# Seeding a PSUM bank with the first product, and interleaving two gated-unit products, in a hedgehog-attention and GLU kernel

## The chip, the core and the metric

The kernel runs on one core of one Trainium2 chip. A core has a matrix engine (TensorE, PE in the profile), a vector engine (VectorE, DVE), a scalar engine (ScalarE, ACT), a general engine (GpSimd, POOL) and a queue engine that issues transfers (SyncE, SP). Matrix products are written to PSUM, which this kernel uses as eight banks of 128 partitions by 512 float32 values. All other tiles lie in SBUF. Each engine works through its own queue in order, and engines wait for each other by semaphores. The metric is the device time of one execution in microseconds; the time of a kernel is the median over runs.

## The reference, cut to what matters

```python
xn = layernorm(x)                                  # x: 2048 tokens x 1024
q, k, v = split_heads(xn @ wqkv)                   # 32 heads of 32
phi_q, phi_k = [concat(softmax(p), softmax(-p)) for p in (q @ w_phi, k @ w_phi)]
o = phi_q (phi_k^T v) / (phi_q (phi_k^T 1) + 1e-6)  # linear attention, per head
s = merge_heads(o) @ wo
h = sigmoid(xn @ w_gate) * (xn @ w_up)             # w_gate, w_up: 1024 x 3584
out = x + s * silu(h @ w_down)
```

All inputs and the result are float32.

## The kernel before, in words

Every large product is computed by a seven-product scheme: both factors are split into 2 x 2 blocks, and seven products of sums of blocks replace eight products of blocks. The seven are named B11, B21, T2, T3, T4, T1, B22 (line 52 and after). With the products written as names, the four blocks of a result are B11 + B21; u1 + T4; u2 + T1; u1 + T1 + B22, where u1 = B11 + T2 and u2 = u1 + T3. Every factor is split into a rounded part and a remainder (`split`: a ScalarE cast, then a VectorE subtraction), and each block product is three matmuls (`mm3`, lines 135 to 137), so that one product over 4 blocks of 128 in the contraction is 12 matmuls of 512 columns into one PSUM bank.

The tokens are worked in two chunks of 1024. For each chunk come first the projections V, K and Q, then the GLU's gate and up products; after both chunks the down products, and at the end the attention output with `wo`. The background work (features of queries, features and key-value sums of keys, the token-major normalization of chunk 1, sums of `wo` and `w_down` blocks) is taken from a list and put, task by task, behind an anchor instruction of the foreground (`background`): a task is planned only after the anchor. In chunk 1 of the GLU a task of key features comes every six products (`k_task`): two transfers, two VectorE reductions and two subtractions (`features`, L446 to L450), an Exp on ScalarE (L451) over 1024 columns, a reduction (L453), a reciprocal (L454), a multiplication (L467), the splits of the features (1024 columns) and of v (512 columns), and a running sum (L476). Its eight matmuls on the key-value banks (L486) are issued before the next task. In chunk 0 of the GLU the tasks are query features and the normalization.

Apart from the opening part (the list `FIRST`) and the last part (`PAIR`), where the order of every engine is written out, a planner sets the order: it takes the instructions in the order of the program and a model of their durations, and gives each engine its queue; a matmul whose operand or bank is not ready by the model is passed by others that are.

In a projection, one product is done for four token tiles, each in a bank of its own (`pbank`). The results are collected by `proj_out`: ScalarE copies B11 out to an SBUF tile u1p and B21's bank out to a result tile; VectorE adds T2's bank onto u1p, and likewise for T3, T4, T1 and B22. T2, T3 and T1 begin anew in the bank; B21, T4 and B22 accumulate on B11, T3 and T1.

In the GLU, one unit (j, s) is a pair of weight column blocks of the gate (s = 0) or of the up matrix (s = 1), and there are 14 x 2 units in a chunk. Its seven products are done in the order B11, T2, B21, T3, T1, T4, B22, with the four opening products B11, T2, T3, T1 each in the next of four banks. B11 is copied out by ScalarE (L1069); T2 (L1071), T3 (L1073) and the last three results (L1081 for the gate, L1088 for up) are added by VectorE; a gate result then goes through ScalarE's sigmoid (L1079 from the bank for B21, L1082 from SBUF for the others), an up result is multiplied with the stored gate, on VectorE for B21 (L1085) and on GpSimd for the other three (L1089). GpSimd then forms the sums of blocks that the down products take, and SP stores them.

The weight operands lie in a ring of eight slots, filled up to eight products ahead (`prep`). `glu_load` loads a unit's raw blocks and `glu_sums` forms their sums on GpSimd; in chunk 0 the split sums are also stored and in chunk 1 loaded back. Both functions are called when the first product of a unit is prepared.

Of the kernel before, what the change touches and what calls it, by code (L numbers as in the profile page):

```python
# [49 lines left out]
def hedgehog_glu_kernel(  # L50
# [77 lines left out]
    def split(o, src):  # L128

        nc.scalar.copy(o[0], src)  # L130
        return nc.vector.tensor_sub(o[1], src, o[0].bitcast(F32))  # L131
# [228 lines left out]
    def prep():  # L360
# [39 lines left out]
    last_evac = []  # L400

    def proj_out(c, which, i, u, b, held=None):
# [12 lines left out]
        def evac(y, x):  # L415
            last_evac[:] = [nc.vector.tensor_add(y, x, b).ins]
# [3 lines left out]
        elif i == B21:  # L420
            y = yp.next()
            nc.scalar.copy(y, b)
            store(0, 0, y)
        elif i == T2:
# [3 lines left out]
        elif i == T4:  # L428
            y = yp.next()
            evac(y, u1p[u])  # L430
            store(0, 1, y)
# [461 lines left out]
    def do_e(o, u):  # L893
        stores[o, u] = []
        proj_out(0, K if o[0] == "K" else V, product(o)[1], int(u), banks[int(u)], stores[o, u])
# [93 lines left out]
    gmm = Ring(banks[:4])  # L989
# [4 lines left out]
    gates = []  # L994
# [22 lines left out]
    for n, (kind, c, what, i) in enumerate(ops):  # L1017
# [3 lines left out]
        if kind == "proj":  # L1021
            for u in range(4):
                if i in opening:
# [3 lines left out]
                for k in range(4):  # L1027
                    mm3(pbank[u], (xo[:, k, 0, us], xo[:, k, 1, us]), pair(ws[k]),
                        i in opening and k == 0, k == 3, skip_group_check=True)
# [6 lines left out]
            if c and n - n1 in EARLY:  # L1036
                background(last_evac[0])
            if (i in (T2, T3, B22)) if c else n in (12, 14, 16, 18):
                with tc.issue_after(last_load[0]):
                    background(last_evac[0], bg2)  # L1040
# [4 lines left out]
        if (j, s, i) == (0, 0, 0):  # L1045
            step(1000)
        if i in opening:
            gbank[i] = gmm.next()
        bank = gbank[{B21: B11, T4: T3, B22: T1}.get(i, i)]
        w = [h.rearrange("p (k m) -> p k m", m=P) for h in pair(ws[0])]  # L1050
        xo = run(XO[i], 4)
        for k in range(4):
            mm3(bank, (w[0][:, k], w[1][:, k]), (xo[:, k, 0], xo[:, k, 1]),
                i in opening and k == 0, k == 3, skip_group_check=True)
# [3 lines left out]
        last_unit = u == len(units) - 1  # L1058
        if flow["item"] == len(items) and flow["made"] - flow["used"] < NW:
            hfree.append(ws[0])  # L1060
            if last_unit and i == 0:
                wfree.extend(range(16, 20))
            while wfree and down_prep():
                pass
        if i == B11:
            u1, u2 = ur.next(), ur.next()
            if s == 0:
                gates = [gates_r.next() for _ in range(4)]
            nc.scalar.copy(u1, bank)  # L1069
        elif i == T2:  # L1070
            v = nc.vector.tensor_add(u1, u1, bank)  # L1071
        elif i == T3:
            v = nc.vector.tensor_add(u2, u1, bank)  # L1073
        else:
            q = {B21: 0, T1: 3, T4: 2, B22: 1}[i]
            g = gates[q]
            if s == 0:
                if q == 0:
                    nc.scalar.activation(g, bank, AF.Sigmoid)  # L1079
                else:  # L1080
                    v = nc.vector.tensor_add(g, u2 if q == 3 else u1, bank)  # L1081
                    nc.scalar.activation(g, g, AF.Sigmoid)  # L1082
            else:
                if q == 0:
                    nc.vector.tensor_mul(g, g, bank)  # L1085
                else:
                    b = u1 if q == 1 else u2
                    v = nc.vector.tensor_add(b, u2 if q == 3 else u1, bank)  # L1088
                    nc.gpsimd.tensor_mul(g, g, b)  # L1089
                if q != 1:  # L1090
                    nc.sync.dma_start(h_d[(B11, None, B21, T4)[q], j, :, c], g)
                else:

                    a11, a21, a12, a22 = gates
# [8 lines left out]
        m = (u % (2 * NJ)) * 7 + glu_order.index(i)  # L1103
        if c == 0:
            if len(bg) > 2 * (TT + 3) and i == T2 and m > 7:
                background(v.ins)
        else:
            if m >= 1 and (m - 1) % 6 == 0:
                background(v.ins)
# [275 lines left out]
```

## Time and profile before

| quantity | value |
|---|---|
| median time of 3 runs | 2378.32 us (2374.84 to 2380.21) |
| profiled execution | span 2376.2 us from first to last instruction; the page gives no other time of it |
| PE busy | 2361.1 us, 99% of the span |
| VectorE busy | 1778.2 us, 75% |
| ScalarE busy | 1022.0 us, 43% |
| GpSimd busy | 959.8 us, 40% |
| granted TensorE clock | 1.000 (mean over the span) |

The profile shows one execution. Busy time of an engine is the union of its instructions' durations; "idle before" is the time that an engine stood still ahead of a group of instructions, with the instruction that released it behind an arrow. A line number like L131 is that of the helper which issues the instruction. Names of tiles are those of the program without numbers: `bank` is a PSUM bank, `w` the weight ring, `fa`, `fb`, `fc` raw and result tiles in SBUF, `p` the split features of keys. Matmuls are pipelined, so a row of 0.39 us can start every 0.23 us.

### The profile page before, as it was taken

Reading aid. Unit: us, or ns where it says so; the run is one execution under the profiler, and the core shown is the slowest. Engines: PE = TensorE matmul, PEld = TensorE weight load, DVE = VectorE, ACT = ScalarE, POOL = GpSimd, SP = SyncE. Lnnn points to the kernel's source line nnn. Section 1 sums busy time; section 2 is a strip of 40 time slices with the busy share of each in tenths; the row PEclk is TensorE's granted clock in tenths of the full one; section 3 lists DMA queues with packets and bytes.
Section 4 is the critical chain, followed back from the end, with each engine's and each line's share of the span. In section 5 each row is a group of like instructions: output and inputs, shape, how many; then the busy total and the mean of one; then the engine's idle time right before and its main releaser. Section 6 shows DMA issues by size and latency. Waiting matters only on the chain.

```text
span 2376.2 us, 31871 instructions
## 1 busy us (share of the span) xinstructions
PE 2361.1 (99%) x10972; PEld 1966.2 (83%) x10972; DVE 1778.2 (75%) x2340; ACT 1022.0 (43%) x1516; POOL 959.8 (40%) x613
## 2 busy tenths in 40 slices
PE   9999999999999999999999999999999999999999
PEld 8888888888888888888878888888888888888887
DVE  8626777877777575668884888865889998878776
ACT  7333344444434342324443444444444334455553
POOL 0223456666666433123443222232333334424566
PEclk9999999999999999999999999999999999999999
DMA  6689987778776787677777666668666666876665
GB/s 237 234 310 321 339 318 263 289 265 291 259 283 246 248 309 261 234 262 242 275 266 250 231 219 216 222 207 312 209 220 230 239 218 209 288 252 244 204 209 177
DMA packets 233587, 600.49 MB, mean 253 GB/s; under 512 B 30672, under 2 KB 30928, under 8 KB 228816
## 3 DMA queue, kind: packets, MB, share of 16 engines
q1 hardware_dynamic: 233424, 598.45, 72.3%
q8 instruction: 86, 1.41, 0.2%
q14 instruction: 77, 0.63, 0.1%
HBM read 363.20 MB, written 235.14 MB: 252 GB/s over the span
## 4 chain that ended last, share of the span: by engine, by line
PE 92%; DVE 4%; DMA 2%; issue 1%; ACT 1%; POOL 0%; SPq 0%; DVEq 0%; ACTq 0%
PE bank L135 29%; PE bank L137 29%; PE bank L136 29%; PE bank L696 1%; PE bank L672 1%; PE bank L486 1%; PE bank L285 1%; DMA fc<-wqkT 1%; DVE p L131 1%; DVE w L131 0%; DVE fc L450 0%; DVE fc L449 0%; DMA x<-x 0%; DMA fa<-wf_d 0%; DVE stk L453 0%
## 5 line engine op out<-in xcount | busy, mean ns | idle before, releaser
L136 PE MATMUL bank<-x,w 128*128 128x512 f32 x2352 | 915.7, 389 | 0.0
L135 PE MATMUL bank<-x,w 128*128 128x512 f32 x2352 | 909.8, 390 | 1.6 <-DVE fc L1073 1.1
L137 PE MATMUL bank<-x,w 128*128 128x512 f32 x2352 | 906.3, 390 | 0.0
L130 ACT CAST w<-fa 128x512 fp32r<-128x512 f32 (+1 forms) x430 | 294.8, 688 | 574.0 <-PE bank L136 365.9
L135 PEld LDWEIGHTS bank<-x,w 128*128 128x128 f32 x2352 | 441.6, 188 | 94.1 <-DVE fc L1073 2.3
L137 PEld LDWEIGHTS bank<-x,w 128*128 128x128 f32 x2352 | 441.5, 188 | 91.5 <-DVE w L131 0.4
L136 PEld LDWEIGHTS bank<-x,w 128*128 128x128 f32 x2352 | 441.6, 188 | 90.3
L131 DVE TENSOR_TENSOR w<-fa,w 128x512 fp32r<-128x512 f32 (+1 forms) x430 | 415.8, 972 | 104.1 <-ACT w L130 90.8
L135 PE MATMUL bank<-w,x 128*128 128x512 f32 x708 | 277.8, 393 | 0.2 <-ACT w L877 0.2
L136 PE MATMUL bank<-w,x 128*128 128x512 f32 x708 | 276.2, 390 | 0.9 <-DVE w L878 0.9
L137 PE MATMUL bank<-w,x 128*128 128x512 f32 x708 | 275.8, 390 | 0.0
L1089 POOL TENSOR_TENSOR fb<-fb,fc 128x512 f32<-128x512 f32 x57 | 89.0, 1561 | 291.6 <-DVE fc L1088 264.8
L137 PEld LDWEIGHTS bank<-w,x 128*128 128x128 f32 x708 | 132.9, 188 | 27.8 <-DVE x L868 0.3
L136 PEld LDWEIGHTS bank<-w,x 128*128 128x128 f32 x708 | 133.1, 188 | 27.4 <-DVE w L878 1.3
L135 PEld LDWEIGHTS bank<-w,x 128*128 128x128 f32 x708 | 133.1, 188 | 27.2 <-ACT w L877 0.6
L628 POOL TENSOR_TENSOR fc<-fc 128x1024 f32<-128x1024 f32 x32 | 81.4, 2542 | 173.7 <-ACT fc L451 125.4
L1088 DVE TENSOR_TENSOR fc<-fc,bank 128x512 f32<-128x512 f32 x84 | 57.5, 684 | 102.5 <-PE bank L137 97.4
L131 DVE TENSOR_TENSOR x<-fa,x 128x512 fp32r<-128x512 f32 x112 | 113.5, 1013 | 23.8 <-ACT x L130 23.6
L130 ACT CAST w<-fb 128x512 fp32r<-128x512 f32 x112 | 69.7, 622 | 141.7 <-PE bank L136 115.3
L131 DVE TENSOR_TENSOR p<-fc,p 128x1024 fp32r<-128x1024 f32 (+2 forms) x97 | 103.9, 1081 | 10.6 <-ACT p L130 8.3
L130 ACT CAST p<-fc 128x1024 fp32r<-128x1024 f32 (+2 forms) x97 | 70.7, 738 | 90.3 <-DVE fc L467 50.7
L640 POOL TENSOR_TENSOR fc<-fc,sa 128x1024 f32<-128x1024 f32 x32 | 70.4, 2199 | 90.6 <-DVE sa L637 90.6
(258 smaller groups left out, 3231.2 us busy)
## 6 DMA issues: line engine op xcount, KB each, us to landing
ws_d<-w SPq DMA_DIRECT2D x112, 512.0 KB, 4.2
w<-ws_d SPq DMA_DIRECT2D x112, 512.0 KB, 4.8
fa<-w_gu SPq DMA_DIRECT2D x84, 512.0 KB, 4.4
fa<-h_d SPq DMA_DIRECT2D x84, 512.0 KB, 4.0
fa<-wf_d SPq DMA_DIRECT2D x32, 1024.0 KB, 6.9
h_d<-fc SPq DMA_DIRECT2D x120, 256.0 KB, 3.2
fc<-e_d SPq DMA_DIRECT2D x48, 512.0 KB, 4.8
fc<-qkv_d SPq DMA_DIRECT2D x80, 256.0 KB, 4.3
```

The costliest lines, as they stand in the source:

```text
L130: nc.scalar.copy(o[0], src)
L131: return nc.vector.tensor_sub(o[1], src, o[0].bitcast(F32))
L135: nc.tensor.matmul(o, a[0], b[0], start=first, stop=False, **kw)
L136: nc.tensor.matmul(o, a[0], b[1], start=False, stop=False, **kw)
L137: nc.tensor.matmul(o, a[1], b[0], start=False, stop=last, **kw)
L285: nc.tensor.matmul(ps[:, gs], r[:, gs], bd[:, 4 * f + g], start=True, stop=True)
L486: nc.tensor.matmul(kvb[g // 2][:, g % 2 * 256:g % 2 * 256 + 256], v[:, g].rearrange("p a f -> p (a f)"), ph[:, g].rearrange("p a f -> p (a ...
L628: nc.gpsimd.tensor_mul(ez, e, zb)
L640: nc.gpsimd.tensor_mul(e3, e3, r2[:, :, None].to_broadcast([P, 32, DH]))
L672: nc.tensor.transpose(ps[:, j * P:(j + 1) * P], e[:, k * P:(k + 1) * P], ident)
L1088: v = nc.vector.tensor_add(b, u2 if q == 3 else u1, bank)
L1089: nc.gpsimd.tensor_mul(g, g, b)
```

## The change

In the projections other than V of chunk 0, ScalarE copies u1p (the value of B11) back into the bank after B21 has been copied out of it. T2, T3 and T4 then accumulate in that bank, and ScalarE copies the bank out after each of them: u1 after T2, u2 after T3, the finished block after T4. Only B11 and T1 begin anew in a bank.

In the GLU the same is done with a copy from one bank to another, ahead of T2. T2, T3 and T4 of all units use one of the four banks; the other three pass from unit to unit (B11 and B21 of a unit, T1 and B22 of a unit, and a free one). T4 is then a finished block in the bank: ScalarE takes the sigmoid of it directly, or VectorE multiplies it with the gate directly. T1 is added on VectorE after u2 is there, B22 after u1. The products of unit k are issued together with the last two products of unit k - 1, in the order B11(k), T4(k-1), B22(k-1), T1(k), T2(k), B21(k), T3(k). Raw weights of the next unit are loaded, and the sums of the current one formed, when T1 is prepared and no longer at B11. The anchor of background tasks is the last VectorE instruction issued, which may now be the subtraction of a split.

```diff
     def split(o, src):
         nc.scalar.copy(o[0], src)
-        return nc.vector.tensor_sub(o[1], src, o[0].bitcast(F32))
+        i = nc.vector.tensor_sub(o[1], src, o[0].bitcast(F32))
+        last_dve[:] = [i.ins]
+        return i
...
-    glu_order = (B11, T2, B21, T3, T1, T4, B22)
+    glu_steps = ((0, B11), (1, T4), (1, B22), (0, T1), (0, T2), (0, B21), (0, T3))
     opening = (B11, T2, T3, T1)
+    fresh = (B11, T1)
...
-        ops += [("glu", c, (j, s), i) for j in range(NJ) for s in range(2) for i in glu_order]
+        ops += [("glu", c, divmod(k - d, 2), i) for k in range(2 * NJ + 1) for d, i in glu_steps if 0 <= k - d < 2 * NJ]
...
-        if i == glu_order[0]:
-            if u % (2 * NJ) == 0:
-                glu_load(u)
+        if i == B11 and u % (2 * NJ) == 0:
+            glu_load(u)
+        if i == T1:
             if (u + 1) % (2 * NJ):
                 glu_load(u + 1)
             glu_sums(u)
...
             y = yp.next()
             nc.scalar.copy(y, b)
             store(0, 0, y)
+            if seeded:
+                nc.scalar.copy(b, u1p[u])
+        elif i == T4:
+            y = yp.next()
+            if seeded:
+                nc.scalar.copy(y, b)
+            else:
+                evac(y, u1p[u])
+            store(0, 1, y)
+        elif seeded and i in (T2, T3):
+            nc.scalar.copy((u1p if i == T2 else u2p)[u], b)
...
-        if i in opening:
-            gbank[i] = gmm.next()
-        bank = gbank[{B21: B11, T4: T3, B22: T1}.get(i, i)]
+        if i == B11:
+            a, b, t2, free = turn
+            turn[:] = free, a, t2, b
+            gbank.update({(u, B11): turn[0], (u, T1): turn[1], (u, T2): turn[2]})
+        bank = gbank[u, {B21: B11, T3: T2, T4: T2, B22: T1}.get(i, i)]
+        if i == T2:
+            nc.scalar.copy(bank, gbank[u, B11])
...
-        if i == B11:
-            u1, u2 = ur.next(), ur.next()
-            if s == 0:
-                gates = [gates_r.next() for _ in range(4)]
-            nc.scalar.copy(u1, bank)
-        elif i == T2:
-            v = nc.vector.tensor_add(u1, u1, bank)
-        elif i == T3:
-            v = nc.vector.tensor_add(u2, u1, bank)
+        if i == T2:
+            us_[u] = ur.next(), ur.next()
+            nc.scalar.copy(us_[u][0], bank)
+        elif i == T3:
+            nc.scalar.copy(us_[u][1], bank)
+        if i in (B21, T4):
+            q = {B21: 0, T4: 2}[i]
+            g = gates[c, j][q]
+            if s == 0:
+                nc.scalar.activation(g, bank, AF.Sigmoid)
+            else:
+                last_dve[:] = [nc.vector.tensor_mul(g, g, bank).ins]
+                nc.sync.dma_start(h_d[(B11, None, B21)[q], j, :, c], g)
+        elif i in (T3, B22):
+            q = {T3: 3, B22: 1}[i]
+            g, y = gates[c, j][q], us_[u][q // 2]
+            if s == 0:
+                last_dve[:] = [nc.vector.tensor_add(g, y, gbank[u, T1]).ins]
+                nc.scalar.activation(g, g, AF.Sigmoid)
+            else:
+                last_dve[:] = [nc.vector.tensor_add(y, y, gbank[u, T1]).ins]
+                nc.gpsimd.tensor_mul(g, g, y)
```

More of the change, by code (lines that the diff above doesn't have):

```diff
@@ L987, in hedgehog_glu_kernel @@
         todo(fold, Q, k)
-    gmm = Ring(banks[:4])
+    turn = banks[:4]
     pbank, gbank = dict(enumerate(banks[:4])), {}
@@ L993, in hedgehog_glu_kernel @@
     hs_r = Ring(halves(48, 49))
-    gates = []
+    gates, us_ = {}, {}
+    glu_begin = [next(n for n, o in enumerate(ops) if o[0] == "glu" and o[1] == c) for c in range(NCH)]
     bg, bg2 = deque(), deque()
@@ new lines, in hedgehog_glu_kernel @@
+        if i == T2:
[3 more added lines that the diff above has]
+            nc.scalar.copy(us_[u][1], bank)
+        if i == B21 and s == 0:
+            gates[c, j] = [gates_r.next() for _ in range(4)]
+        if i in (B21, T4):
+            q = {B21: 0, T4: 2}[i]
+            g = gates[c, j][q]
+            if s == 0:
+                nc.scalar.activation(g, bank, AF.Sigmoid)
[5 more added lines that the diff above has]
+            g, y = gates[c, j][q], us_[u][q // 2]
+            if s == 0:
+                last_dve[:] = [nc.vector.tensor_add(g, y, gbank[u, T1]).ins]
[3 more added lines that the diff above has]
+                nc.gpsimd.tensor_mul(g, g, y)
+                if q == 3:
+                    nc.sync.dma_start(h_d[T4, j, :, c], g)
+                else:
+                    a11, a21, a12, a22 = gates[c, j]
```

55 lines of the change are left out of this document (16 added, 39 removed).

## The prediction

> **What bounds the kernel now.** I read the page first: its first part, then the chain that ended last.
>
> ```profile
> span 2376.2 us, 31871 instructions
> ...
> PE 2361.1 (99%) x10972; PEld 1966.2 (83%) x10972; DVE 1778.2 (75%) x2340; ACT 1022.0 (43%) x1516; POOL 959.8 (40%) x613
> ...
> PE 92%; DVE 4%; DMA 2%; issue 1%; ACT 1%; POOL 0%; SPq 0%; DVEq 0%; ACTq 0%
> ```
>
> TensorE is idle for 2376.2 - 2361.1 = 15.1 us of the span, and its matmuls are the same after the change. So the change can save only idle time, and cost by adding some. Where the idle time lies is told by the busy time by stage (columns: length, then busy us of PE, PEld, DVE, ACT, POOL, then clock, DMA share, GB/s) and by the waits of PE:
>
> ```profile
> 300.00:800.00 500.00, 500.00 (x2215) 413.76 (x2214) 380.16 (x506) 216.21 (x320) 310.98 (x211) 1.00 0.77 277
> 1100.00:1250.00 150.00, 146.57 (x673) 121.25 (x671) 127.27 (x146) 68.40 (x86) 63.34 (x41) 1.00 0.77 263
> 1250.00:1600.00 350.00, 349.77 (x1611) 291.54 (x1610) 258.81 (x329) 151.55 (x207) 102.86 (x69) 1.00 0.67 226
> 2110.00:2376.00 266.00, 260.71 (x1395) 220.28 (x1393) 198.77 (x276) 132.67 (x231) 134.82 (x94) 1.00 0.64 214
> ```
>
> ```profile
> PE bank L486 <- DVE p L131: 2.1, 2, 1.2
> PE bank L285 <- DMA fc<-wqkT: 2.1, 3, 1.6
> PE bank L942 <- POOL ident masks.py:199: 1.5, 1, 1.5
> PE bank L135 <- DVE fc L1073: 1.1, 2, 0.9
> PE bank L136 <- DVE w L878: 0.9, 1, 0.9
> ...
> PE bank L135 <- DVE fb L1081: 0.4, 1, 0.4
> ```
>
> The GLU of chunk 0 (300 to 800 us) has no idle PE at all, that of chunk 1 (1100 to 1600) has 3.43 + 0.23 = 3.7 us, in which PE waited for VectorE: 2.1 us at the key-value products (L486), 1.1 + 0.4 us at evacuations of T3 and of the later products. The clock is 1.00 throughout, so nothing is to be had there. The rest, 5.3 us in the last stage among it, lies where the diff changes no line.
>
> **The unit of time.** The rows of PE and VectorE in the GLU give the pace:
>
> ```profile
> 501.11 0.39 PE L137 MATMUL bank<-x,w 128*128 128x512 f32 x1
> 501.34 0.39 PE L135 MATMUL bank<-x,w 128*128 128x512 f32 x1
> ...
> 501.61 0.69 DVE L1071 TENSOR_TENSOR fc<-fc,bank 128x512 f32<-128x512 f32 x1 [0.91 <-PE bank L137]
> ```
>
> A matmul starts every 500 / 2215 = 0.226 us, so a product of 12 takes 2.72 us. The product that ended with the first row was evacuated 0.27 us after the next product's first matmul started. I count from that start; an evacuation begins at 0.27.
>
> **What is removed and moved.** Counted in the two kernels' queues: VectorE loses 200 tensor-tensor instructions, ScalarE gains 192 copies and 8 table loads, GpSimd loses 28 multiplications; transfers and matmuls keep their numbers. The prices are these groups, by shape:
>
> ```profile
> L130 ACT CAST w<-fa 128x512 fp32r<-128x512 f32 x84 | 52.1, 621 | 112.7 <-PE bank L136 112.5 <-DMA h_d<-fb 0.2
> L130 ACT CAST p<-fc 128x1024 fp32r<-128x1024 f32 x26 | 27.5, 1056 | 47.0 <-DVE fc L467 47.0
> L1069 ACT COPY fc<-bank 128x512 f32<-128x512 f32 x26 | 15.1, 579 | 4.7 <-PE bank L137 4.6
> L1079 ACT ACTIVATE fb<-bank 128x512 f32<-128x512 f32 x9 | 5.4, 600 | 0.2
> L1082 ACT ACTIVATE fb<-fb 128x512 f32<-128x512 f32 x27 | 17.1, 632 | 16.3 <-DVE fb L1081 16.2
> ...
> L1088 DVE TENSOR_TENSOR fc<-fc,bank 128x512 f32<-128x512 f32 x41 | 28.1, 685 | 51.6 <-PE bank L137 50.3 <-POOL fc L1089 1.2
> L131 DVE TENSOR_TENSOR p<-fc,p 128x512 fp32r<-128x512 f32 x29 | 27.8, 958 | 0.2
> L449 DVE TENSOR_TENSOR fc<-fc,stk 128x512 f32<-128x512 f32 x25 | 27.7, 1109 | 0.0
> ```
>
> VectorE sheds 200 x 0.685 = 137 us (75% to 69% of the span), ScalarE takes on 192 x 0.58 + 8 x 1.28 (its row stands below) = 122 us (43% to 48%). Neither bounds the kernel, so neither total enters the sum: what counts is who must finish before PE may write a bank. A copy by ScalarE into PSUM has no row. The nearest are its copy out of a bank, 0.579, and its cast between SBUF tiles, 0.621; I take 0.60, being between close ends.
>
> **The projections: nothing.** T2 of a token tile now needs two ScalarE copies after B21 (the stored result, then the seed), where one evacuation was enough. Between B21 and T2 of one tile lie the other three tiles, 3 x 2.72 = 8.2 us; the work for four tiles, 8 x 0.6 and two casts of 1.06 (the 1024-column price), is 6.9 us of a product's 10.9. Without that cover each of five projections would wait 0.6 us for its first seed, 3 us in all.
>
> **The GLU: one bank, short windows.** Before, four banks rotated, and B11's was written anew only four products, 10.9 us, after B21's end. Now T2, T3, T4 of every unit run in one bank. In PE's queue of the changed kernel a step is mostly T2, B21, B11', T3, T1', T4, B22, T2' (' is the next unit). So T4 must wait for ScalarE's copy of T3, with one product, T1', as cover; and T2' for T4's evacuation and then the seed, with one product, B22. In the plain case T4's evacuation on VectorE ends at 0.27 + 0.69, the seed at about 1.7: 1 us is left of 2.72. That is why chunk 0 costs nothing. But ScalarE takes its queue in order, and in chunk 1 the key features (L446 to L476) put an Exp and its dependents between these copies. One of them as it ran before:
>
> ```profile
> 1306.02 1.28 ACT L451 ACT_TABLE_LOAD   x1
> 1312.41 1.06 ACT L451 ACTIVATE fc<-fc 128x1024 f32<-128x1024 f32 x1 [5.11 <-DVE fc L450]
> 1313.49 1.28 ACT L1079 ACT_TABLE_LOAD   x1
> 1314.79 0.60 ACT L1079 ACTIVATE fb<-bank 128x512 f32<-128x512 f32 x1
> ...
> 1316.46 1.06 ACT L130 CAST p<-fc 128x1024 fp32r<-128x1024 f32 x1 [0.57 <-DVE fc L467]
> ```
>
> ```profile
> 1306.27 0.68 DVE L446 TENSOR_REDUCE stk<-fc 128x16 f32<-128x512 f32 x1
> 1306.87 0.68 DVE L447 TENSOR_REDUCE stk<-fc 128x16 f32<-128x512 f32 x1
> ...
> 1313.51 1.22 DVE L453 TENSOR_REDUCE stk<-fc 128x32 f32<-128x1024 f32 x1 [0.53 <-ACT fc L451]
> 1314.76 0.35 DVE L454 RECIPROCAL stk<-stk 128x32 f32<-128x32 f32 x1
> 1315.15 1.22 DVE L467 TENSOR_TENSOR fc<-fc,stk 128x1024 f32<-128x1024 f32 x1
> ```
>
> ScalarE stood 5.11 us behind an Exp, and PE lost nothing. With the new windows it would. Reading the changed ScalarE and VectorE queues of chunk 1, three kinds of step put this chain in front of a bank that PE needs. A hand-over between engines is put at 0.1.
>
> Kind one (4 steps): T3's copy, load, Exp, load, sigmoid, cast of v, cast of the keys (1024 columns), T4's sigmoid, seed. From T3's end: a cast and T3's copy end at 0.27 + 0.62 + 0.58 = 1.47; load and Exp at 3.8; load and sigmoid at 5.7; cast of v 6.4; VectorE's v part and then L467 end at 6.5 + 0.96 + 1.22 = 8.7; key cast 9.8; sigmoid and seed 11.1; PE 11.2. Allowed are T1', T4, B22 and the eight key-value products that stand among them, 8.16 + 1.2 = 9.4. It is 1.8 late, or 0.6 if v's part ran beside the loads; I take 1.5, near the upper end, since the queue puts v's part ahead of L467: 6.0 us.
>
> ```profile
> 1114.01 1.21 PE bank L486 x8
> ```
>
> Kind two (3 steps): after B21 a load, sigmoid, load and Exp (0.27 + 1.28 + 0.60 + 1.28 + 1.06 = 4.5), then reduce and reciprocal to 6.1, v's part to 6.9, L467 to 8.2, key cast 9.3, T3's copy 9.9, PE 10.0, against B11', T3, T1' and a set of key-value products, 9.4: 0.6 each, between 0 and 0.8; 1.8 us.
>
> Kind three (3 steps): T3's copy, load, Exp, seed. VectorE has seven instructions and then L453 ahead of T4's multiplication. At its pace of 0.60 (1306.27 to 1306.87) PE gets the bank at 9.75, at mean durations like 958 and 1109 ns at 11.4; allowed is 10.0, as two thirds of B11' run after T3 here. Between 0 and 1.4, I take 0.7: 2.1 us.
>
> Three steps in which the key-value sums are closed have more on ScalarE; bounded by 0 and 2.5 us for the longest, I put 2 us on all. The relief of VectorE gives back some of its waits, between 0 and 2.1 + 1.1 + 0.4 = 3.6 us; I take 2.5, as the T3 evacuation it was waited for is gone. Loads of gate and up weights are now issued four products (10.9 us) before they are needed, not seven; they land in 4.4 us, so this costs nothing; a late one would hold T3's copy behind its cast. SP's store of T4's result now follows VectorE rather than GpSimd, one engine less; no load waits for it, so nothing. At a chunk's end the last T4 and B22 have no next unit; in PE's queue products of the next stage stand between them, so nothing; without those, two waits of about 1.5 us (T3's copy, from kind one) in each chunk, 6 us.
>
> ```profile
> fa<-w_gu SPq DMA_DIRECT2D x84, 512.0 KB, 4.4
> ```
>
> Sum: 6.0 + 1.8 + 2.1 + 2.0 - 2.5 = +9.4 us. On the profiled span that is 2385.6; the median shown, 2378.32, is 2.1 above that span (the page gives no other time of that execution), so I predict 2388 us. No change that a measurement of this kernel can tell is within 0.2%, 4.8 us.
>
> **Rivals.** First, all windows hold (23%): kinds two and three reach zero at their low ends, and kind one needs only v's part earlier. Then 2378.3, less up to 3.6 us of VectorE's waits: 2375 to 2378, no change. Second, ScalarE waits for VectorE as long as before (14%):
>
> ```profile
> ACT L451 <- DVE fc L450: 28.2, 17, 3.0
> ACT fc L451 <- DVE fc L450: 20.9, 5, 5.1
> ```
>
> That is 49.1 us over 26 Exp, 1.9 us each; if half of it reaches PE, another 25 us, 2413. Against it stands VectorE's lighter load. Third, the other sign (10%): VectorE's queue gets short enough that every Exp has its input before T3 ends; then no step stalls, the 3.6 us of waits go, and the 2.1 us behind wqkT may: 2378.3 - 5.7 = 2372.6. It decides if, in kind one, v's part runs before the sigmoid. Against it: in chunk 1 VectorE was 127.27 of 150 us busy.
>
> The fourth (3%): each table load is followed by a wait of its length. In the rows, the load starts 0.02 us after the Exp's end (1313.47) and the sigmoid 0.02 after the load's, so there is none. [...]
>
> **Chances.** My forecast 50%, with its own range 2381 to 2398, of which 5% falls below 2383. Slower 0.45 + 0.14 + 0.03 = 0.62; same 0.23 + 0.05 = 0.28; faster 0.10. The range goes from 2374 (most of the third rival lies below) to 2406 (the upper half of the second and fourth above).
>
> **What would show it.** PE's waits in 1100 to 1600 us should name ScalarE's copies and the seed, in some ten steps, by 0.5 to 2 us each, with PE's idle time there near 13 us, not 3.7; the chunk-0 GLU should stay without idle PE; the waits behind T3 evacuations on VectorE should be gone. Seeds late in chunk 0 too would mean that the plain window is shorter than I worked out; PE idle at the projections' T2, that their cover is gone. If chunk 1 shows less than 3.7 us, the third rival holds.

## The result, and the profile after

The changed kernel takes 2420.68 us (median of 4 runs, 2417.11 to 2426.36) against 2379.2 us (4 runs): a ratio of 1.0184, 95% interval 1.0171 to 1.0196. It is slower by 41.5 us, outside the predicted 2374 to 2406 us; the sign was right. The profiled execution is the slowest of the four: it took 2426.36 us with a span of 2424.6, 48.4 more than the span before, so the profile shows some 6 us more than the median.

The page of the kernel after: the span, the busy times and the chain that ended last.

```profile
span 2424.6 us, 31622 instructions
...
PE 2381.1 (98%) x10972; PEld 1976.1 (82%) x10972; DVE 1657.4 (68%) x2140; ACT 1130.6 (47%) x1716; POOL 917.4 (38%) x585
...
PE 81%; DVE 6%; DMA 5%; ACT 3%; issue 3%; POOL 2%; SPq 1%; DVEq 0%; ACTq 0%; POOLq 0%
```

VectorE lost 120.8 us (1778.2 to 1657.4) and ScalarE gained 108.6 (1022.0 to 1130.6), where 137 and 122 were counted. PE's idle time rose from 15.1 to 43.5 us, which is 28.4 of the 48.4. The other 20.0 are PE's own busy time: the same 10972 matmuls took longer. Busy time by stage, first of before, then of after (the last row of each is the GLU of chunk 1; columns as in the prediction, clock after POOL):

```profile
288.00:868.00 580.00, 580.00 (x2567) 479.86 (x2566) 437.37 (x558) 255.68 (x370) 339.17 (x227) 1.00 0.77 278
1046.00:1661.00 615.00, 611.34 (x2802) 508.43 (x2802) 457.97 (x575) 265.12 (x362) 192.46 (x126) 1.00 0.71 245
```

```profile
290.00:877.00 587.00, 582.60 (x2554) 478.55 (x2555) 381.80 (x481) 309.68 (x451) 309.39 (x211) 1.00 0.76 271
1055.00:1718.00 663.00, 636.65 (x2848) 526.20 (x2848) 435.81 (x514) 287.51 (x417) 186.23 (x114) 0.97 0.69 230
```

In chunk 1's GLU PE is idle for 663.00 - 636.65 = 26.4 us, not 3.7, and the granted clock is 0.97. PE's waits name what was forecast, only longer (columns: us in total, times, the longest):

```profile
PE bank L139 <- ACT bank L1065: 15.6, 5, 3.7
PE bank L139 <- ACT fc L1084: 8.6, 4, 4.0
PE bank L139 <- ACT w L130: 3.1, 1, 3.1
PE bank L139 <- DVE fb L1099: 2.8, 2, 1.9
```

L1065 is the seed, L1084 the copy of T3, L1099 VectorE's addition of T1 for the gate. To see where the 48 us come from without stage borders, I count matmuls: the delay of the n-th matmul against the n-th of the profile before (good to a few us inside the GLU, where the orders differ). The gains in delay between fixed n, in us, for the kernel after and for the runs told below:

| run | up to 232 us | to 325 (start of chunk 0's GLU) | to 1046 | to 1661 (chunk 1's GLU) | to the end | sum |
|---|---|---|---|---|---|---|
| after | -3.6 | +9.1 | +5.3 | +37.5 | +0.1 | +48.4 |
| p1_proj_only | -1.1 | +1.4 | +2.2 | -0.6 | -0.2 | +1.7 |
| p2_glu_only | -1.2 | +4.7 | +4.8 | +34.0 | +0.3 | +42.6 |
| x1_copy | -2.5 | +7.3 | +5.8 | +19.2 | +1.5 | +31.2 |
| x1_no_exp | -1.8 | +4.4 | +5.9 | +13.3 | +3.4 | +25.2 |
| x3_behind_seed | -2.1 | +7.9 | +3.1 | +16.8 | +0.1 | +25.8 |
| x4_behind_t3 | -2.6 | +7.5 | +1.3 | +47.9 | +1.5 | +55.6 |
| x5_wo_early | -2.9 | +1.1 | +5.3 | +37.8 | 0.0 | +41.3 |
| x6_seed_kv | -1.4 | +1.1 | +1.9 | +19.8 | +0.7 | +22.1 |
| x7_raw_keys | -4.3 | +4.6 | +4.3 | -4.3 | +0.6 | +1.0 |
| x8_no_sums | -2.7 | +7.9 | +4.4 | +0.2 | +1.4 | +11.2 |
| x9_wd_odd | -4.3 | +1.1 | +4.6 | +8.7 | +0.8 | +10.9 |
| after_again | -3.1 | +7.9 | +4.5 | +38.7 | +0.7 | +48.7 |

A step of kind one in the kernel after. First ScalarE, then VectorE, then GpSimd in the same stretch, then PE (start, us, engine, instruction, in brackets the idle time before it and what ended it):

```profile
1121.98 0.58 ACT L1084 COPY fc<-bank 128x512 f32<-128x512 f32 x1
1127.66 1.28 ACT L461 ACT_TABLE_LOAD   x1 [5.10 <-DVE fc L460]
1128.95 1.06 ACT L461 ACTIVATE fc<-fc 128x1024 f32<-128x1024 f32 x1
...
1134.42 1.05 ACT L130 CAST p<-fc 128x1024 fp32r<-128x1024 f32 x1 [1.95 <-DVE fc L477]
1135.37 0.59 ACT L1091 ACTIVATE fb<-bank 128x512 f32<-128x512 f32 x1
1135.99 0.57 ACT L1065 COPY bank<-bank 128x512 f32<-128x512 f32 x1
```

```profile
1117.96 2.21 DVE L486 TENSOR_TENSOR fc<-fc 128x1024 f32<-128x1024 f32 x1
1120.09 2.31 DVE L131 TENSOR_TENSOR p<-fc,p 128x1024 fp32r<-128x1024 f32 x1
1122.33 1.77 DVE L131 TENSOR_TENSOR w<-fa,w 128x512 fp32r<-128x512 f32 x1
1124.02 0.67 DVE L456 TENSOR_REDUCE stk<-fc 128x16 f32<-128x512 f32 x1
...
1125.21 0.68 DVE L459 TENSOR_TENSOR fc<-fc,stk 128x512 f32<-128x512 f32 x1
1125.80 1.77 DVE L460 TENSOR_TENSOR fc<-stk,fc 128x512 f32<-128x512 f32 x1
1127.50 1.76 DVE L131 TENSOR_TENSOR w<-fa,w 128x512 fp32r<-128x512 f32 x1
1129.18 0.67 DVE L1099 TENSOR_TENSOR fb<-fc,bank 128x512 f32<-128x512 f32 x1
```

```profile
1117.35 1.74 POOL L583 TENSOR_TENSOR fb<-fb 128x512 f32<-128x512 f32 x1 [0.50 <-DMA fb<-w_down]
1119.05 2.27 POOL L1112 TENSOR_TENSOR fc<-fb 128x512 f32<-128x512 f32 x1
1121.28 2.27 POOL L584 TENSOR_TENSOR fb<-fb,fb 128x512 f32<-128x512 f32 x1
1123.51 1.75 POOL L1113 TENSOR_TENSOR fc<-fc 128x512 f32<-128x512 f32 x1
1125.22 1.81 POOL L585 TENSOR_TENSOR fb<-fb,fb 128x512 f32<-128x512 f32 x1
1127.11 1.60 POOL L586 TENSOR_TENSOR fb<-fb 128x512 f32<-128x512 f32 x1
```

```profile
1129.91 0.50 PE L139 MATMUL bank<-x,w 128*128 128x512 f32 x1 [1.85 <-DVE fb L1099]
1136.62 0.80 PE L139 MATMUL bank<-x,w 128*128 128x512 f32 x1 [3.69 <-ACT bank L1065]
```

Exp has to wait 5.10 us, and everything behind it in ScalarE's queue, the seed last, moves with it. The durations on VectorE are to be compared with those in the prediction's rows: there 512 columns took 0.68 us and 1024 columns 1.22; here a subtraction of 512 columns takes 1.77 and an instruction on 1024 columns 2.21 to 2.31. Four such stand ahead of Exp: 0.99 + 1.09 + 2 x 1.09 = 4.3 us of excess, most of the 5.10. All run while GpSimd is busy. The reduction beside it (L456, 0.67) is not slowed. The addition from a bank (L1099, 0.67) ran here with GpSimd idle; in this GLU of the kernel before, all 15 such additions of T2 and T3 (L1071, L1073) that ran with GpSimd busy throughout took 0.67 to 0.69. Nor is every instruction with two SBUF operands slowed: L459 took 0.68 although GpSimd was at work by its row. But neither L459 nor L460 is slowed without GpSimd: with it idle throughout, they took 0.68 to 0.69 us in all 37 instances of this GLU.

### The profile page after: what moved, and what is told of

Same layout as the page of the kernel before. It is cut to its first block, busy times and chain, and to the rows that moved or that the text cites. A ratio compares the mean times of both kernels' runs of the same rounds, so it can differ in the third digit from the quotient of the medians.

```text
span 2424.6 us, 31622 instructions
## 1 busy us (share of the span) xinstructions
PE 2381.1 (98%) x10972; PEld 1976.1 (82%) x10972; DVE 1657.4 (68%) x2140; ACT 1130.6 (47%) x1716; POOL 917.4 (38%) x585
## 4 chain that ended last, share of the span: by engine, by line
PE 81%; DVE 6%; DMA 5%; ACT 3%; issue 3%; POOL 2%; SPq 1%; DVEq 0%; ACTq 0%; POOLq 0%
PE bank L139 25%; PE bank L140 25%; PE bank L141 25%; DVE w L131 1%; PE bank L706 1%; PE bank L682 1%; DVE p L131 1%; PE bank L496 1%; DMA fc<-xo_d 1%; DMA fc<-wo 1%; DMA fa<-wf_d 1%; DVE fc L477 1%; PE bank L289 1%; ACT fc L461 1%; DVE fc L460 1%
## 5 line engine op out<-in xcount | busy, mean ns | idle before, releaser
L139 PE MATMUL bank<-x,w 128*128 128x512 f32 x2352 | 923.2, 393 | 30.8 <-ACT bank L1065 15.6
L140 PE MATMUL bank<-x,w 128*128 128x512 f32 x2352 | 921.7, 392 | 0.0
L141 PE MATMUL bank<-x,w 128*128 128x512 f32 x2352 | 919.8, 392 | 1.2 <-DVE w L131 1.2
L131 DVE TENSOR_TENSOR w<-fa,w 128x512 fp32r<-128x512 f32 (+1 forms) x430 | 432.8, 1015 | 310.3 <-ACT w L130 291.6
L1103 POOL TENSOR_TENSOR fb<-fb,fc 128x512 f32<-128x512 f32 x38 | 58.5, 1539 | 344.1 <-DVE fc L1102 344.0
L131 DVE TENSOR_TENSOR w<-fb,w 128x512 fp32r<-128x512 f32 x112 | 97.7, 877 | 37.4 <-ACT w L130 37.3
```

The source lines that it names most:

```text
L131: i = nc.vector.tensor_sub(o[1], src, o[0].bitcast(F32))
L139: nc.tensor.matmul(o, a[0], b[0], start=first, stop=False, **kw)
L140: nc.tensor.matmul(o, a[0], b[1], start=False, stop=False, **kw)
L141: nc.tensor.matmul(o, a[1], b[0], start=False, stop=last, **kw)
L1103: nc.gpsimd.tensor_mul(g, g, y)
```

## The experiments

**Which half.** The projections of after with the GLU of before, and the other way round: the branch for `glu_order` and the banks from the one kernel, `proj_out` and `fresh` from the other.

```diff
-    glu_steps = ((0, B11), (1, T4), (1, B22), (0, T1), (0, T2), (0, B21), (0, T3))
+    glu_order = (B11, T2, B21, T3, T1, T4, B22)        # p1_proj_only
...
-    def proj_out(c, which, i, u, b, held=None, seeded=True):
+    def proj_out(c, which, i, u, b, held=None, seeded=False):        # p2_glu_only
```

> Seeding in the projections alone, with the GLU as before. Two theories. The queue theory puts the loss on ScalarE's queue in the GLU (an Exp that waits for VectorE stands ahead of the copies that free PE's bank): then this kernel is within 0.2% of before, 2375 to 2381 us, with some 3 us gained in the first 235 us (the changed kernel's matmuls stood 3.6 us earlier there) and up to 3 us lost where the projections of chunk 1 begin. The rival, that the additional copies of the projections are a good part of the loss, gives 2385 us or more.

> Seeding and interleaving in the GLU alone, with the projections as before. The queue theory expects nearly the whole loss: 2412 to 2428 us, 35 us or more of it between 1050 and 1660 us. The rival, that projections and GLU share the loss, gives 2400 us or less.

Measured: projections alone 2378.21 us, ratio 1.0002 (0.9993 to 1.0011); GLU alone 2423.61, ratio 1.0192 (1.0176 to 1.0209). Both times lie in the queue theory's ranges; chunk 1's GLU lost 34.0 us, just short of the 35 expected. The loss is the GLU's. No run takes seeding, interleaving and the later loading of weights in the GLU apart.

**Exp and its table loads.** In the key tasks Exp is replaced by a copy, or left out. Of the 99 table loads in the profile of the kernel after, 1.28 us each, none stands directly ahead of a copy.

```diff
-        nc.scalar.activation(e, e, AF.Exp)
+        nc.scalar.copy(e, e)        # x1_copy; in x1_no_exp the line is gone
```

> The changed kernel, with a copy in place of the Exp of the key features: the instruction waits for VectorE as before and takes about as long, but needs no table load, so the loads ahead of Exp and sigmoid go. The features are then not exponentiated, so the keys' sums are other numbers. If the wait for VectorE is what counts, it stays at 2405 to 2425 us. If the table loads (1.28 us each, two in a step) are what counts, it falls to 2385 to 2400 us.

> The changed kernel with the Exp of the key features left out altogether (the keys' sums are then other numbers), so that ScalarE never waits for VectorE's subtractions. The queue theory expects the waits of 2 to 4 us in the GLU of chunk 1 to vanish and with them the half clock behind them: 2382 to 2395 us, the 9 us lost where the GLU of chunk 0 begins staying. The window theory (one bank with one product as cover is too short whatever stands in the queue) expects 2408 us or more.

Measured 2409.0 (ratio 1.0126, 1.0108 to 1.0144) and 2404.12 (1.0115, 1.0096 to 1.0134). The copy's time lies in the range of the theory that the wait for VectorE counts; the time without Exp lies between its two theories. The loss of chunk 1's GLU goes from 37 us to 19 and 13: so Exp and its loads lengthen the chain too, but a third of the loss comes about without any Exp. PE's waits without Exp still name the seed, and VectorE's addition more than before (5.2 us in place of 2.8):

```profile
PE bank L139 <- ACT bank L1066: 7.0, 5, 2.4
PE bank L139 <- DVE fb L1100: 5.2, 3, 1.9
```

**The place in the queue.** All key tasks of chunk 1's GLU at one place of the step. In the kernel after they come every sixth product of seven, at each place in turn.

```diff
-    EARLY = (4, 7, 11, 14, 18)
+    EARLY = tuple(range(2, 21, 2))
...
             nc.scalar.copy(bank, gbank[u, B11])
+            if c:
+                background(last_dve[0])        # x3_behind_seed
...
-            if m >= 1 and (m - 1) % 6 == 0:
+            if i == T3:        # x4_behind_t3
                 background(last_dve[0])
```

> The kernel after, with the key tasks of chunk 1's GLU at one fixed place, right behind the seed (in the kernel after they come every sixth product, so at each of the seven places in turn); the five tasks for which 28 steps have no room move into chunk 1's projections. Theory one, the place in ScalarE's queue decides: Exp with its loads and its wait for VectorE now stands ahead of the copy of T2, which has some 8 us until it is due, so most of the 37 us lost in this GLU come back; 2385 to 2398 us. Rival, the one-bank windows do not bear a key task at any place: it stays within 6 us of the kernel after, 2414 or more, with waits at other copies.

> As the run with the tasks behind the seed, but the place is behind T3's product, so that every Exp stands ahead of a seed, the place at which the kernel after lost 3.8 us and 2.5 us more at half clock in four steps. Theory one: 22 or so such steps at 4 to 6 us, 90 to 130 us more than the kernel before, and about 11 us more for what is lost elsewhere: 2475 to 2520 us, PE waiting almost only for the seed. Rival (the place does not matter, it is the load of VectorE): 2410 to 2435.

Measured 2405.0 (ratio 1.0113, 1.0097 to 1.0129) and 2433.53 (2 runs, 1.0232, 1.021 to 1.0254). The place matters: the same tasks cost 16.8 us at one place and 47.9 at the other. But both times miss theory one; x3 lies between the two theories, x4 inside the rival's range. Waits of PE, x3 and then x4:

```profile
PE bank L496 <- DVE p L131: 9.7, 3, 3.9
```

```profile
PE bank L139 <- ACT bank L1065: 30.6, 14, 3.5
```

Behind T3 the seed was late in 13 steps of this GLU, not in 22 (the 14th of the row is at the start of chunk 0's GLU). Later than 1300 us it was every second step, at 44 us of distance, though every step had its Exp ahead of the seed. Behind the seed, PE waited at three places for VectorE's split of the key features. Something that is not in every step makes VectorE late. In x3 around 1170 us, VectorE and GpSimd:

```profile
1174.29 1.75 DVE L131 TENSOR_TENSOR w<-fa,w 128x512 fp32r<-128x512 f32 x1
1175.95 2.28 DVE L131 TENSOR_TENSOR p<-fc,p 128x1024 fp32r<-128x1024 f32 x1
1178.16 0.68 DVE L131 TENSOR_TENSOR w<-fa,w 128x512 fp32r<-128x512 f32 x1
```

```profile
1173.24 2.24 POOL L585 TENSOR_TENSOR fb<-fb,fb 128x512 f32<-128x512 f32 x1
1175.56 1.59 POOL L586 TENSOR_TENSOR fb<-fb 128x512 f32<-128x512 f32 x1
```

The same subtraction takes 1.75 us beside GpSimd and 0.68 a moment after GpSimd's last. GpSimd's sums of gated values come at the end of every up unit, so in every second step. At the three places where PE waited for the split, the four sums of a task on the down projection's weights (L583 to L586) ran between and behind these; later, beside the sums of gated values alone, these products waited 0.06 us at most.

**The key-value products later, and no features.** The first puts PE's key-value products of the x3 kernel behind B21 of the step that plans their task, not of the next one as the expectation says. At this GLU's first step two tasks fall due together, and the older takes the newer's features. The second leaves the features out.

```diff
+        if bg_glu and i == T3:
+            kv_products()        # x6_seed_kv; and products 10, 12, 14, 16 as in x5_wo_early
```

```diff
-        r = features(f"k{t}{hb}", kraw, e_k)
-        e3 = e_k.rearrange("p (g d) -> p g d", d=DH)
-        nc.vector.tensor_mul(e3, e3, r[:, :, None].to_broadcast([P, 32, DH]))
+        raw = whole(52)        # x7_raw_keys: split and summed in place of e_k
```

> The kernel with the key tasks behind the seed, with two more moves: the key-value products of a task come behind B21 of the next step in place of right behind its seed (there PE waited 9.7 us in three places for the casts of p), and the four tasks on the output projection's weights come two products earlier. If the 16.7 us that were left in chunk 1's GLU are these waits and the half clock behind them, and the 8 us at the start of chunk 0's GLU go as in the run with the early tasks, then 2384 to 2393 us. Rival (what is left in this GLU is the one-bank windows' own): 2396 or more.

> The kernel after, with the key tasks' features left out: the raw keys and values are split and summed, so that of a task two casts by ScalarE and two subtractions and a sum by VectorE stay, and its Exp, the reductions, the subtractions ahead of Exp and the key's multiplication are gone (the keys' part of the result is not computed). If VectorE's load is what is left without Exp (13 us in chunk 1's GLU), the loss there falls to 4 us or less, and with the 11 us elsewhere the time is 2388 to 2396. If the windows fail by the casts themselves, about as without Exp, 2400 to 2406.

x6: 2401.78 (ratio 1.0095, 1.0073 to 1.0117), in the rival's range, its waits for the split 11.6 us in three places. It tells nothing on its question, because the products did not move: the planner lets others pass a product whose features are late, and at all three places they stand behind as many matmuls as in x3 (5149, 5333 and 5873 from the start) and the same late split. x7: 2384.84 (10 runs, 2379.06 to 2387.86; ratio 1.0022, 1.0011 to 1.0033), some 3 us below what was expected. The table takes its profiled execution, the fastest of the ten. There chunk 1's GLU gains 4.3 us on the kernel before, at full clock:

```profile
1055.00:1718.00 663.00, 662.53 (x3032) 552.16 (x3031) 317.69 (x382) 229.28 (x387) 189.20 (x121) 1.00 0.73 244
```

So the interleaving itself, one bank and short windows, cost nothing there; it is the features that did not fit.

**GpSimd's sums taken away.** The key tasks stay whole, with Exp and its table loads, where the kernel after has them; of GpSimd's work the sums shown are left out, in all fourteen tasks on the down projection's weights and in chunk 1's GLU.

```diff
-        sub(b11, b12, b11)
-        sub(b12, b22, b12)
-        sub(b22, b22, b11)
-        sub(b21, b21, b22)
...
+                    s3, s2, s4 = a11, a12, a22
+                    if c == 0:
                         s3, s2, s4 = [hs_r.next() for _ in range(3)]
                         nc.gpsimd.tensor_sub(s3, a11, a21)
                         nc.gpsimd.tensor_add(a21, a21, a22)
                         nc.gpsimd.tensor_sub(s2, a21, a11)
                         nc.gpsimd.tensor_sub(s4, a12, s2)
```

> The kernel after, with GpSimd's subtractions and additions of chunk 1's GLU left out: the four that make the down projection's sums of gated values and the four of each task on the down projection's weights (unsummed blocks are stored in their place, so those products get wrong operands). In the kernel after, VectorE's instructions with two operands in SBUF take 0.68 us while GpSimd is idle and 1.78 while it is busy (1.22 and 2.20 for 1024 columns); those from a bank and the reductions do not change. Theory: Exp comes late, and with it the sigmoid and the seed behind it, because the key task's VectorE work runs beside GpSimd's sums. Then these instructions take 0.68 and 1.22 us throughout, the loss in chunk 1's GLU falls from 37 us to 15 or less, and the time is 2385 to 2399 us. Rival (Exp with its two table loads, 3.6 us, does not fit the window anyway): 25 us or more stay, 2408 or more.

Measured 2389.25 (ratio 1.005, 1.0035 to 1.0065), in the theory's range, and the loss of chunk 1's GLU is 0.2 us. Through this GLU the queues of PE, VectorE and ScalarE hold the same instructions in the same order in both kernels, so no other order of the planner's is behind it. Groups by shape between 1046 and 1661 us, the kernel after and then x8 (busy us, mean ns; the reduction, 1.20 to 1.22 us in the kernel after with GpSimd busy or idle, is there for comparison):

```profile
L477 DVE TENSOR_TENSOR fc<-fc,stk 128x1024 f32<-128x1024 f32 x28 | 38.3, 1366 | 0.7
...
L463 DVE TENSOR_REDUCE stk<-fc 128x32 f32<-128x1024 f32 x28 | 34.1, 1219 | 27.1 <-ACT fc L461 27.1
L460 DVE TENSOR_TENSOR fc<-stk,fc 128x512 f32<-128x512 f32 x28 | 29.0, 1036 | 0.0
```

```profile
L477 DVE TENSOR_TENSOR fc<-fc,stk 128x1024 f32<-128x1024 f32 x28 | 34.2, 1222 | 0.7
L463 DVE TENSOR_REDUCE stk<-fc 128x32 f32<-128x1024 f32 x28 | 34.2, 1220 | 32.5 <-ACT fc L461 32.5
...
L460 DVE TENSOR_TENSOR fc<-stk,fc 128x512 f32<-128x512 f32 x28 | 19.1, 682 | 0.0
```

And the same step as shown above, now with Exp's input there after 0.37 us and PE's wait down from 3.69 us to 1.10:

```profile
1120.80 0.58 ACT L1079 COPY fc<-bank 128x512 f32<-128x512 f32 x1
1121.74 1.28 ACT L461 ACT_TABLE_LOAD   x1 [0.37 <-DVE fc L460]
...
1130.07 0.57 ACT L1060 COPY bank<-bank 128x512 f32<-128x512 f32 x1
```

```profile
1130.69 0.50 PE L139 MATMUL bank<-x,w 128*128 128x512 f32 x1 [1.10 <-ACT bank L1060]
```

This settles the cause: GpSimd's sums, running beside the key features, make many of VectorE's instructions with two SBUF operands take up to 1.8 us for 0.7. The kernel before has the same slow instructions (in this GLU 9 of the 27 of L450 took 1.77 to 1.78 us, the 18 with GpSimd idle 0.68 to 0.69); there little behind them was due at PE (3.7 us of waits in this GLU). GpSimd's multiplications of gate and up stay in x8, and 6 of the 28 splits of 1024 columns beside them still took 2.31 us.

**A move that leaves nothing out.** The x3 kernel, with the two kinds of sum tasks shifted.

```diff
-            if (i in (T2, T3, B22)) if c else n in (12, 14, 16, 18):
+            if (i in (T2, T3, B22)) if c else n in (10, 12, 14, 16):        # x5_wo_early too
...
-            if m >= 14 and m % 14 == 0:
+            if m >= 14 and m % 14 == 7:
```

> The kernel with the key tasks behind the seed, its four tasks on the output projection's weights two products earlier, and the tasks on the down projection's weights in the GLU seven products later, so that GpSimd's four sums of such a task do not follow the four of the gated values; nothing is left out. In the run with the tasks behind the seed, PE waited 9.7 us in three places for the casts of p, all while these tasks still ran (before 1310 us), and hardly later. If GpSimd's two bursts one behind the other are the cause, these waits go, and with 8 us less at the start of chunk 0's GLU the time is 2382 to 2392 us. Rival (one burst is enough, or the place of the tasks is): 2395 or more.

Measured 2389.73 (ratio 1.0059, 1.0037 to 1.0081), inside theory one's range: 31 of the 41 us are back with all work done, about half of it by the place behind the seed (x3) and half by the two shifts. PE's waits for the split fell from 9.7 us to 5.1 (5 times, the longest 1.6). The four longest, 0.91 to 1.65 us, come where a task's sums on the down projection's weights now run alone, late in VectorE's chain; beside the sums of gated values alone the wait was 0.05 us at most. So one burst at that place is still too much. No run beats the kernel before: what x7 gained in this GLU, 4 us, comes without the features only.

**The start of chunk 0's GLU.** The last task on the output projection's weights moved ahead.

> The kernel after, with the four tasks that sum blocks of the output projection's weights behind chunk 0's products 10, 12, 14 and 16 in place of 12, 14, 16 and 18. If the 9 us lost at the start of chunk 0's GLU come from the last of these tasks (its cast waited 5.96 us for GpSimd at the head of ScalarE's queue, with the GLU's weight casts behind it), they mostly come back: 2409 to 2415. If the start of the interleaved GLU itself is the cause, no change: 2418 or more.

In the kernel after, a cast of that task held ScalarE's queue, with the GLU's weight casts behind it:

```profile
287.37 0.62 ACT L130 CAST p<-fc 128x512 fp32r<-128x512 f32 x1 [5.96 <-POOL fc L239]
```

In the trace of x5 the loss there is 1.1 us in place of 9.1, as expected, and so it is in those of x6 and x9, which have the same shift. But the time is 2419.14 (2415.96 to 2420.84, ratio 1.017, 1.0151 to 1.0188), inside the second theory's range. The shift is shown to remove these waits in the profiled executions; that it brings 8 us in every execution is not.

**The clock.** Two runs, one of before with waits added, one of after unchanged.

```diff
+        grade = GRADES.get(u) if i == T1 and c == 0 else None
+        if grade:
+            nc.scalar.copy(bank, gbank[T3])
+            for _ in range(grade - 1):
+                nc.scalar.copy(bank, bank)
```

> The kernel before, with waits of graded length put ahead of T1 in 19 steps of chunk 0's GLU: one to eight copies of 128x512 by ScalarE into its bank, about 0.57 us each (the bank's first value is written by T1 itself, so nothing is computed differently). It is to show from which length on a wait of PE is followed by half clock. Reading of the kernel after: none up to 2.0 us, sometimes at 2.0 to 2.3, always from 3.8 on; each drop costs 1.7 to 2.7 us. Then some 8 to 11 drops and 2415 to 2450 us. Rival (the drop needs something else than PE's own wait, such as ScalarE and VectorE busy at once): drops that do not go with the length of the wait, or none.

> The kernel after, unchanged. All half-clock periods seen so far start on one grid of 3.413 us, and the first of each follows a stretch between two lines of the grid in which PE stood still for 1.85 us or more (none below 1.82). If so, the same waits give another number of half-clock periods when the grid lies otherwise: waits as before within 1 us in all, periods 5 to 9, and a span that differs from the first by the difference in slowed matmuls (1.7 to 2.7 us each). Rival (the length of the wait alone decides): the same places drop.

clock_graded took 2524.94 us, well above what was expected: the copies stood behind other work of ScalarE, and the waits came out at 3.2 to 8.7 us, three of them broken in two pieces of 2.1. All 19 were followed by half clock (0.976 granted over the span; behind a wait of 3.25 us matmuls started every 0.43 us), so the run gives no lower end. after_again took 2423.6 (2420.51 to 2426.65). Its waits at the seed and the copy of T3, 14.0 + 9.0 us, are close to 15.6 + 8.6, and it has 8 periods of half clock where the first profile has 7; the spans differ by 0.2 us. The granted clock is 0.992 in both. The same places drop in both, as the rival has it, and one more, at 1267 us, where another wait had grown from 0.93 to 1.86 us. So this pair settles nothing. What decides is seen within the first profile, whose half-clock periods begin whole multiples of 3.413 us apart, within 0.001 us: in stretches of 3.41 us between the lines of that grid (the borders printed lie up to 0.06 us ahead of its lines; PE's busy time stands after the length, the clock third from the end):

```profile
1128.09:1131.50 3.41, 1.59 (x7) 1.33 (x8) 3.19 (x4) 3.37 (x4) 0.62 (x1) 1.00 0.89 243
1131.50:1134.92 3.42, 1.42 (x7) 0.84 (x5) 2.54 (x4) 1.47 (x3) 0.00 (x0) 1.00 0.59 176
1134.92:1138.33 3.41, 1.71 (x4) 1.43 (x5) 2.40 (x3) 2.25 (x4) 0.00 (x0) 0.50 0.87 344
1138.33:1141.74 3.41, 3.41 (x9) 2.64 (x9) 0.00 (x0) 0.03 (x1) 0.00 (x0) 0.50 0.01 5
...
1564.95:1568.37 3.42, 2.33 (x11) 1.60 (x9) 3.35 (x5) 1.57 (x3) 0.00 (x0) 1.00 0.81 267
1568.37:1571.78 3.41, 2.38 (x10) 1.99 (x11) 3.41 (x5) 2.26 (x3) 0.00 (x0) 1.00 0.40 137
```

PE idle 1.82 us of the first stretch: no effect. Idle 2.00 of the second: the next two run at half clock, and the one of them without a wait holds 9 matmuls, where 3.41 us at 0.227 hold 15. In the last two a wait of 2.12 us is cut by a line of the grid into 1.08 and 1.03 (1.15 and 0.97 at the line itself, 1568.43): no effect, while the same 2.12 us in one piece at 1438.77 us halved the clock. The length of the wait alone, the rival, cannot tell these two apart.

## Why the prediction was wrong

**What held.** PE is the bound (busy for 98% of the span); the counts of moved instructions; the projections cost nothing (1.0002). ScalarE's copies and the seed are what PE waits for, as forecast, and the places are the steps of kinds one and two. The waits behind VectorE's evacuation of T3 are gone, so that relief came. In the step shown no table load was followed by a wait of its length: the second load, 1.28 us from 1130.03, has the sigmoid behind it at 1131.32.

**Where it failed: the size of kinds one and two.** Kind one was put at 1.5 us with Exp's input ready when ScalarE reached it ("load and Exp at 3.8"). Measured are 3.69, 3.65, 3.65 and 3.65 us, and 1.85 and 0.93 us in two of these steps for VectorE's L1099, which the prediction did not have: 17.4 in place of 6.0. Kind two, T3's copy, was put at 0.6 and bounded by 0.8; measured are 4.03, 2.12 and 2.12, together 8.3 in place of 1.8. Kind three and the closing steps, 4.1 us forecast, cost less than 1. The step that failed is this "load and Exp at 3.8": it lets Exp's load start when T3's copy ends, 1.47 us after T3, and so puts ScalarE's wait for VectorE's subtractions at nothing, in kind two as well. In the step shown this wait was 5.10 us. The rows that say otherwise were quoted: Exp 5.11 us behind L450, and L449 at a mean of 1109 ns, where a reduction of as many elements takes 0.68 us. I used that mean as one end for kind three alone and did not ask why it was so long. It is long because GpSimd runs beside some of its instances: between 1046 and 1661 us the 15 with GpSimd idle took 0.68 to 0.69 us, the 12 others 0.69 to 1.78. With GpSimd's sums out (x8), kind one waits 0.75 to 1.10 us and the rest nothing, near the forecast. The 0.1 put for a hand-over between engines was an estimate; in the step shown the seed ended at 1136.56 and PE's matmul started at 1136.62.

**What was left out: the clock.** The working priced a wait at its own length ("cost by adding some" idle time), and matmuls that take longer were not in it. Waits that left PE idle for 1.96 us or more of one stretch of the grid cost more: in chunk 1 the matmuls behind them lost some 15 us at half clock (37.5 us of delay less 26.4 - 3.7 = 22.7 of added idle time), two fifths of the loss. Counted by matmul in the six periods of half clock there, it is 12.6 us: 8 to 13 matmuls in each, that start every 0.427 us in place of 0.227.

**What was left out: the seam.** The start of chunk 0's GLU, 4 to 9 us in the profiles without the shift, was not looked at; inside chunk 0's GLU the forecast of no cost was near (about 2.5 us, in four steps of 0.6, each at a wait of 0.3 us at L551); 2.8 us more came where it passes into chunk 1's projections.

**The rivals.** The second, ScalarE waiting for VectorE as long as before, was the right mechanism, with a 14% chance: Exp and its loads waited 27.7 + 20.9 = 48.6 us for L460 in the kernel after, where it was 49.1 before. Its price, half of 49.1 us at 2413, put 25 us on waits, and 22.7 us of idle time came. But the half was a guess, and neither the clock nor the start of chunk 0's GLU was in it, so that it is only 8 us short is in part luck. "VectorE's lighter load" does not speak against it: the load that counts is the slowed instructions ahead of Exp, and the change took away others, from a bank (L1071, L1073), which took 0.67 to 0.69 us beside GpSimd too. The fourth rival, which the upper end of the range counts in, rests on a wait behind each table load that no run shows; behind the second load of the step shown the sigmoid started after 0.01 us.

## What to carry to other kernels

When a change shortens the time a bank may be held, take each wait of the engine that frees it at its present length, and ask for the worst step what stands ahead on the engine that it waits for. If one instruction has two durations in a trace, find out which other engine is busy in the slow instances before you put a mean into a sum. And a stall of the matrix engine is to be priced with the clock behind it: 2.12 us of waiting cost nothing more here when it fell into two stretches of the clock's grid, and halved the clock when it fell into one.

## What was not expected of the hardware

VectorE beside GpSimd, in chunk 1's GLU of the kernel after. With both operands in SBUF, the split of 512 columns of weights took 0.68 to 0.69 us with GpSimd idle throughout and 1.77 to 1.79 with it busy throughout, the split of 1024 columns of features 1.22 to 1.23 and 2.30 to 2.31, the running sum of as many 1.22 to 1.23 and 2.20 to 2.21. Not every instance is slowed: two of L459 took 0.68 with GpSimd busy throughout. The reductions took 0.67 to 0.68 (512 columns) and 1.20 to 1.22 (1024), with GpSimd busy or idle. Additions with one operand in a bank took 0.67 to 0.69 with GpSimd busy throughout, 15 in the kernel before and one in the kernel after.

The clock, in the kernel after. Its seven periods of half clock inside the span begin on one grid of 3.413 us, within 0.001 us, and last one or two of its stretches (3.413 or 6.827 us). Every one follows a stretch in which PE was idle for 1.96 us or more, and no stretch at full clock with 1.85 us or less is followed by one. That is the reading of one profile; the expectation of after_again has 1.85 as enough, from the profiles up to then. The idle times rest on modelled ends of matmuls, so the limit is good to some hundredths. A period cost 1.5 to 2.6 us of slower matmuls.

ScalarE's copy from one bank to another took 0.572 us in the mean of 56 in the kernel after, no more than its copy from a bank to SBUF (0.579, L1084).
